# First-product weight operands: whole-unit loads into two rotating buffers, or piecewise loads into two fixed halves

## The chip, the cores and the metric

One Trainium2 chip, one of its cores. The metric is the device time of one launch in microseconds (us). TensorE is called PE here, VectorE DVE, ScalarE ACT, GpSimd POOL, and SyncE, which issues nearly all transfers of this kernel, SP.

## What is computed

Windowed attention over 4 x 8 heads of 576 x 64, whose output, as x of 2304 tokens x 512, goes through a mixture of 8 experts with Sinkhorn-normalised routing weights, and that through a feed-forward layer with the activation h cos(h). All in float32.

```python
attn = softmax(scale * q @ k.T + bias, causal window 128); x = attn @ v
P = exp(x @ w_gate - max)
for _ in range(8):
    P /= P.sum(1) + 1e-9
    P /= P.sum(0) + 1e-9
    P *= N / E
for e in range(8):
    out += P[:, e:e+1] * (relu(x @ w1[e]) @ w2[e])
h = out @ w_in
result = (h * cos(h)) @ w_out
```

## The kernel before, in words

The tokens are cut into three blocks of 768. After the attention the kernel runs 120 steps, one for each unit of 256 hidden columns in each block: 32 expert units for block 0, the same 32 for block 1 and for block 2 (kind "moe", b = 0, 1, 2), and 8 units of the feed-forward layer for each of the three blocks (kind "ffn").

Each unit has a first product (x by a slice of w1, or of w_in) and a second one (the hidden values by a slice of w2, or of w_out). The first product is a 2 x 2 block product in Strassen-Winograd form, with seven products numbered 1 to 7. `unit_mm` (L846) issues one of them: six matmuls of 128 x 384, since each operand is a pair of float32r numbers, high and low part, and three pairings are needed for each of two inner chunks. The left operands of the seven products, as high and low parts, are the tile `wa`: 14 KB in each partition, 1792 KB in all. The pool `wp` gives two buffers that rotate from unit to unit.

In block 0 the operands are made on the chip: `prep_s` (L126) forms four sums on POOL, `prep_a` (L136) copies the high parts on ACT, subtracts the low parts on DVE, and stores the whole tile into a DRAM scratch `wd1[u]` (L147). For the ffn units `prep_ffn` (L194) does the same in pieces during the later expert blocks and stores each piece into `wd1[u]` (L216). In blocks 1 and 2 and in all ffn steps, `wa` is loaded back from that scratch: `load_w(u, b, "a")` (L120), one transfer for a unit.

The order is written out by hand. The main loop (L1134) runs over the steps and within a step over the products in the order 5, 1, 4, 2, 3, 6, 7; at the place of product 4 the previous unit's product 4 is issued, which is its last. Right behind it `begin(n + 1)` (L1086) calls `load_w` for the next step, so that load waits until the previous unit's last product has read its buffer.

The second product of block 0 and of ffn is `g2` (L1064), 36 matmuls at the place marked 0 between products 6 and 7. For blocks 1 and 2 the second product is itself done in Strassen-Winograd form over pairs of units: `s_step` (L973) issues six matmuls behind each product (`couple`, L1026), and every second call issues on SP a load of 512 KB into one of the four parts of `wbX` (L1013), three products of that chain ahead. What it loads was made in block 0 by `prep_b` (L155) and `prep_sb` (L171), which forms the combinations of w2 on POOL (L181), splits them on ACT (L184) and DVE (L186) and stores them (L189). `prep_sb` is a generator: `slot()` (L1129, L1179, L1181) takes one piece of the first generator in the list `sbq`, which starts as `[prep_sb(0), prep_sb(1)]` (L1115); later units are appended by `begin_b` (L1098). A step of block 0 offers five slots, and five more in the batch of `g2` once there is one.

Behind the products, `product` (L862) drains the banks with ACT copies (`keep`, L881) and DVE additions (L884), and weighs the hidden values with the routing row by DVE (L899); that row is a broadcast load, one for four units (`load_p`, L797). The results of `s_step` are added up on DVE (L997) and its right operands split by ACT (L1009) and DVE (L1005). In blocks 1 and 2 the ffn weights are also converted in the background (`convert_f64`, L253, and `prep_ffn`), with loads and stores on SP.

SP issues its transfers in program order: one that waits for a semaphore holds those behind it.

## Time and profile before

| what | value |
|---|---|
| median of 3 runs | 2079.3 us (2074.7 to 2088.33) |
| the profiled execution's own time | 2079.26 us |
| its span | 2077.5 us |
| mean granted PE clock | 0.992 |
| PE busy | 2008.0 us |
| DVE, ACT, POOL busy | 1608.7, 869.5, 888.4 us |
| moved by transfers | 538.96 MB, mean 259 GB/s |

The span is what the profiler saw between first and last instruction. Busy time counts an engine as busy while an instruction of it is under way. [...] Block 0 lies between about 200 and 690 us of the span, block 1 from 700 to 1181, block 2 to 1670, the ffn stage behind.

### The profile page before, as it was taken

The page shows a single profiled execution, that of the slowest core. Times are in us where ns is not written, and L with a number is a line of the kernel's source. Part 1 is how long each engine was busy: PE and PEld are TensorE (multiplying, and loading weights), DVE is VectorE, ACT ScalarE, POOL GpSimd, SP SyncE. Part 2 cuts the span into 40 slices and gives each one's busy share as a digit, 9 for nine tenths or more (in the row PEclk, how much of TensorE's full clock was granted, in tenths as well). Part 3 has the DMA queues.
Part 4 walks back from the last instruction along what each step waited for, and adds up shares of the span by engine and source line. Part 5 has one row for each costly group of instructions (what it writes and reads, how often), then busy time and mean ns, then how long its engine had stood idle before and what let it go on. Part 6 is the DMA issues. An engine that isn't in the chain of part 4 may idle for free.

```text
span 2077.5 us, 30570 instructions
## 1 busy us (share of the span) xinstructions
PE 2008.0 (97%) x10960; PEld 1853.6 (89%) x10960; DVE 1608.7 (77%) x2714; ACT 869.5 (42%) x1639; POOL 888.4 (43%) x780
## 2 busy tenths in 40 slices
PE   8989899999999999999999999999999999999998
PEld 6656789989989899999999999999999998898897
DVE  6765787777777788878898878798887886857765
ACT  6776334444444343333333333233332345454443
POOL 5444356666657343343445332344352414223222
PEclk9999999999999999999999999999999999999999
DMA  6634578888888798878989678897888664455552
GB/s 162 189 69 120 209 274 297 306 314 296 308 309 304 254 336 314 316 281 322 327 312 338 261 270 291 301 336 282 333 319 279 240 244 184 170 218 198 203 188 107
DMA packets 236216, 538.96 MB, mean 259 GB/s; under 512 B 71872, under 2 KB 147744, under 8 KB 217632
## 3 DMA queue, kind: packets, MB, share of 16 engines
q1 hardware_dynamic: 236064, 537.00, 72.3%
q8 instruction: 87, 1.43, 0.3%
q14 instruction: 65, 0.53, 0.1%
HBM read 383.27 MB, written 153.67 MB: 258 GB/s over the span
## 4 chain that ended last, share of the span: by engine, by line
PE 81%; DVE 7%; DMA 7%; issue 2%; ACT 1%; POOL 1%; SPq 0%; POOLq 0%; ACTq 0%; DVEq 0%
PE gT L985 19%; PE y_moe L852 17%; PE z_moe L852 9%; PE gT L1073 6%; PE gT L1071 6%; PE gT L1072 6%; DMA wa<-wd 6%; PE y_ffn L852 4%; PE x_moe L852 4%; PE s L494 2%; PE z_ffn L852 2%; PE x L586 2%; PE x_ffn L852 1%; DVE hX L1005 1%; PE T L458 1%
## 5 line engine op out<-in xcount | busy, mean ns | idle before, releaser
L985 PE MATMUL gT<-hX,wbX 128*128 128x384 f32 x2688 | 543.0, 336 | 5.6 <-DVE acc_moe L997 3.1
L985 PEld LDWEIGHTS gT<-hX,wbX 128*128 128x128 f32 x2688 | 474.6, 189 | 10.8 <-DVE acc_moe L997 5.9
L852 PE MATMUL y_moe<-xtT_moe,wa 128*128 128x384 f32 x1728 | 347.0, 335 | 0.6 <-ACT s_moe L881 0.6
L852 PEld LDWEIGHTS y_moe<-xtT_moe,wa 128*128 128x128 f32 x1728 | 304.4, 188 | 3.3 <-ACT s_moe L881 0.9
L997 DVE TENSOR_TENSOR acc_moe<-gT,acc_moe 128x384 f32<-128x384 f32 x432 | 237.4, 550 | 88.7 <-PE gT L985 87.5
L1071 PE MATMUL gT<-wbX,hX 128*128 128x512 f32 x672 | 264.4, 393 | 8.2 <-ACT hX L802 4.3
L1073 PE MATMUL gT<-wbX,hX 128*128 128x512 f32 x672 | 264.4, 393 | 4.6 <-POOL hX L840 2.9
L1072 PE MATMUL gT<-wbX,hX 128*128 128x512 f32 x672 | 264.0, 393 | 0.0
L881 ACT ACTIVATE s_moe<-y_moe 128x384 f32<-128x384 f32 x192 | 93.5, 487 | 348.2 <-PE y_moe L852 348.2
L1018 POOL TENSOR_TENSOR cX<-cX 128x768 f32<-128x768 f32 x64 | 123.3, 1927 | 214.3 <-DVE hX L1005 125.6
L1018 POOL TENSOR_TENSOR hodd<-hodd 128x768 f32<-128x768 f32 x64 | 131.2, 2049 | 195.6 <-DVE hX L1005 109.7
L840 POOL TENSOR_TENSOR hX<-cX,hX 128x768 fp32r<-128x768 f32 x48 | 93.0, 1952 | 267.7 <-ACT hX L838 238.2
L133 POOL TENSOR_TENSOR s<-ra 128x256 f32<-128x256 f32 x80 | 61.5, 769 | 235.6 <-DVE wa L145 161.2
L1071 PEld LDWEIGHTS gT<-wbX,hX 128*128 128x128 f32 x672 | 127.2, 189 | 35.9 <-ACT hX L802 4.7
L1062 DVE SCALAR_TENSOR_TENSOR acc_moe<-gT,prob,acc_moe 128x512 f32<-128x512 f32 x174 | 129.9, 748 | 37.7 <-PE gT L1073 36.6
L1073 PEld LDWEIGHTS gT<-wbX,hX 128*128 128x128 f32 x672 | 127.0, 189 | 32.7 <-POOL hX L840 3.7
L1072 PEld LDWEIGHTS gT<-wbX,hX 128*128 128x128 f32 x672 | 127.2, 189 | 25.2
L1005 DVE TENSOR_TENSOR hX<-cX,hX 128x768 fp32r<-128x768 f32 x112 | 148.2, 1323 | 0.9 <-ACT hX L1009 0.9
L1005 DVE TENSOR_TENSOR hX<-hodd,hX 128x768 fp32r<-128x768 f32 x112 | 142.3, 1271 | 0.0
L852 PE MATMUL z_moe<-xtT_moe,wa 128*128 128x384 f32 x576 | 120.4, 343 | 21.8 <-DMA wa<-wd 16.5
L802 ACT ACTIVATE hX<-cX 128x768 fp32r<-128x768 f32 x64 | 44.0, 688 | 231.8 <-DVE cX L884 231.8
L852 PEld LDWEIGHTS z_moe<-xtT_moe,wa 128*128 128x128 f32 x576 | 102.7, 192 | 27.1 <-issue 7.3
(181 smaller groups left out, 3815.7 us busy)
## 6 DMA issues: line engine op xcount, KB each, us to landing
wa<-wd SPq DMA_DIRECT2D x88, 1792.0 KB, 7.4
wbX<-wdp SPq DMA_DIRECT2D x224, 512.0 KB, 8.0
wd<-wa SPq DMA_DIRECT2D x32, 1792.0 KB, 6.8
wdp<-sb SPq DMA_DIRECT2D x32, 1024.0 KB, 6.1
wdp<-wbX SPq DMA_DIRECT2D x96, 256.0 KB, 4.4
wbX<-wd SPq DMA_DIRECT2D x24, 1024.0 KB, 4.8
ra<-in_moe_w_dram SPq DMA_DIRECT2D x64, 256.0 KB, 7.4
rb<-in_moe_w_dram SPq DMA_DIRECT2D x64, 256.0 KB, 4.3
```

The lines of the kernel that those rows point to most:

```text
L133: nc.gpsimd.tensor_tensor(out=s4[:, o], in0=x, in1=y, op=op)
L840: nc.gpsimd.tensor_tensor(out=h[:, 1], in0=c, in1=h[:, 0].bitcast(F32), op=ALU.subtract)
L852: nc.tensor.matmul(ps[:, :HB], wa[:, wl, WI[m], kc, :], x[:, xl, kc, :], start=start and kc == 0 and n_ == 0, stop=stop and kc == 1 and n_ ...
L881: nc.scalar.activation(out=t["s", i], in_=ps[:, :HB], func=AF.Copy)
L985: nc.tensor.matmul(ps[:, :HB], w[:, u, wl, d * P:(d + 1) * P], x[:, xl, u, :], start=m in (1, 5, 2) and n_ == 0, stop=m in (4, 3, 2) and n ...
L997: nc.vector.tensor_tensor(out=a, in0=ps[:, :HB], in1=a, op=ALU.add)
L1005: nc.vector.tensor_tensor(out=x[:, 1], in0=H[:, q], in1=x[:, 0].bitcast(F32), op=ALU.subtract)
L1018: nc.gpsimd.tensor_tensor(out=H[:, t[0]], in0=H[:, t[1]], in1=H[:, t[2]], op=ALU.subtract)
L1062: nc.vector.scalar_tensor_tensor(out=a, in0=ps, scalar=pe, in1=a, op0=ALU.mult, op1=ALU.add)
L1071: nc.tensor.matmul(ps, hf[f][:, 0, ts], wb[:, f, 0, :], start=f == 0, stop=False)
L1072: nc.tensor.matmul(ps, hf[f][:, 0, ts], wb[:, f, 1, :], start=False, stop=False)
L1073: nc.tensor.matmul(ps, hf[f][:, 1, ts], wb[:, f, 0, :], start=False, stop=f == 1)
```

## The change

`wa` is no longer a rotating tile. One fixed tile `waX` holds two halves, for even and odd units, and each half holds the seven operands one after the other, with their high and low parts together (before: all high parts, then all low parts). The scratch in DRAM has the same order. A unit's operands are loaded in four transfers: those of products 5 and 1, of 2 and 3, of 6 and 7 (512 KB each) and of 4 (256 KB). When a product has been issued that frees the places of such a transfer, the transfer for the unit that uses this half next, two units on, is put down, and it is issued behind the product that follows. `begin` no longer loads. The operands of products 5 and 1 lie in places 3 and 0, of 2 and 3 in places 1 and 6, of 6 and 7 in 4 and 5, of product 4 in place 2. Besides, `prep_sb(1)` is not in the list from the start but appended at the beginning of the second step.

```diff
-    wp = ctx.enter_context(tc.tile_pool(name="wp", bufs=2))
+        waX = ring.tile([P, 2, 7 * 4 * P], F32R, name="waX")
-        def load_w(u, b, ab):
-            t = new_w(u, b, ab)
-            if ab == "a":
-                nc.sync.dma_start(out=flat_a(t), in_=wd1[u])
+        WI = {1: 0, 2: 1, 4: 2, 5: 3, 6: 4, 7: 5, 3: 6}
+        def wa_of(u):
+            return waX[:, u % 2].rearrange("p (o h k f) -> p o h k f", o=7, h=2, k=2)
+        def load_a(u, ms):
+            o = sorted(WI[m] for m in ms)
+            o = slice(o[0], o[-1] + 1, o[-1] - o[0] or 1)
+            out = waX[:, u % 2].bitcast(F32).rearrange("p (o w) -> p o w", o=7)
+            nc.sync.dma_start(out=out[:, o], in_=wd1[u].rearrange("p (o w) -> p o w", o=7)[:, o])
...
-            parts = [(wa[:, :, 0:2], both), (wa[:, :, 2], ra[:, 2:4, P:]), (wa[:, :, 3:7], s4)]
+            parts = [(wa[:, 0:2, 0], wa[:, 0:2, 1], both), (wa[:, 2, 0], wa[:, 2, 1], ra[:, 2:4, P:]),
+                     (wa[:, 3:7, 0], wa[:, 3:7, 1], s4)]
...
-            pieces = [(x, w1d[:, :, o], 2) for o, x in enumerate(ops)]
+            pieces = [(x, w1d[:, o], 2) for o, x in enumerate(ops)]
...
-                        ps[:, :HB], wa[:, wl, WI[m], kc, :], x[:, xl, kc, :],
+                        ps[:, :HB], wa[:, WI[m], wl, kc, :], x[:, xl, kc, :],
...
-                if b or kind == "ffn":
-                    load_w(u, b, "a")
-                elif u >= 2:
+                if kind == "moe" and not b and u >= 2:
                     pre.append(prep_a(u))
...
-        sbq += [prep_sb(0), prep_sb(1)]
+        sbq.append(prep_sb(0))
+        fetch = []
+        AHEAD = {1: (2, (5, 1)), 3: (2, (2, 3)), 7: (2, (6, 7)), 4: (1, (4,))}
...
+            if (kind, b, u) == ("moe", 0, 1):
+                sbq.append(prep_sb(1))
...
                     begin(n + 1)
                 else:
                     product(s, m)
+                while fetch:
+                    load_a(*fetch.pop(0))
+                if m in AHEAD:
+                    d, ms = AHEAD[m]
+                    if n + d < len(steps) and steps[n + d][:2] != ("moe", 0):
+                        fetch.append((steps[n + d][2], ms))
                 tick()
```

The loads of `wbX` for the ffn units move into a function `load_b` of their own, unchanged in place and size.

## Rows read from the trace of the kernel before

**Rows 1.** The page, busy time of PE: us, share of the span, instructions.

```profile
PE 2008.0 (97%) x10960; PEld 1853.6 (89%) x10960; DVE 1608.7 (77%) x2714; ACT 869.5 (42%) x1639; POOL 888.4 (43%) x780
```

**Rows 2.** Table: stretch, length, busy by engine, granted clock, DMA share, GB/s.

```profile
700.00:1181.00 481.00, 468.75 (x2638) 462.00 (x2637) 403.35 (x584) 164.13 (x291) 198.10 (x139) 0.98 0.84 311
...
286.00:680.00 394.00, 394.00 (x1985) 357.33 (x1984) 303.80 (x407) 174.46 (x284) 258.95 (x233) 1.00 0.86 306
1710.00:2050.00 340.00, 336.63 (x1685) 303.08 (x1684) 231.00 (x323) 166.52 (x251) 99.73 (x52) 1.00 0.52 188
```

**Rows 3.** Idle before wa's readers; PE's waits: us in total, times, longest.

```profile
  DMA wa<-wd: 17.0, 11
...
PE gT L985 <- DVE acc_moe L997: 3.1, 5, 1.0
...
PE gT L985 <- DMA wbX<-wdp: 0.5, 1, 0.5
```

**Rows 4.** Timelines of PE and SP, transfers of one window: two stalls, one load.

```profile
741.46 1.30 PE L852 MATMUL z_moe<-xtT_moe,wa 128*128 128x384 f32 x6 [0.89 <-DVE hodd L884]
...
1524.05 1.28 PE L852 MATMUL z_moe<-xtT_moe,wa 128*128 128x384 f32 x6 [0.93 <-DVE cX L899]
...
1513.79 0.32 SPq L120 DMA_DIRECT2D wa<-wd  x1
...
wa<-wd SPq DMA_DIRECT2D x1, 1792.0 KB, 10.1
```

**Rows 5.** SP's wait for wa; transfers: count, KB each, median us to landing.

```profile
SPq L120 <- PE y_moe L852: 314.7, 64, 11.3
...
wa<-wd SPq DMA_DIRECT2D x88, 1792.0 KB, 7.4
wbX<-wdp SPq DMA_DIRECT2D x224, 512.0 KB, 8.0
...
wd<-hla SPq DMA_DIRECT2D x48, 256.0 KB, 7.7
```

**Rows 6.** Timeline of PE around the longest stall: start, us, instructions, idle before.

```profile
843.65 1.34 PE L985 MATMUL gT<-hX,wbX 128*128 128x384 f32 x6 [0.97 <-DVE acc_moe L997]
844.83 1.20 PE L852 MATMUL y_moe<-xtT_moe,wa 128*128 128x384 f32 x6
845.87 1.20 PE L985 MATMUL gT<-hX,wbX 128*128 128x384 f32 x6
849.97 2.26 PE L852 MATMUL z_moe<-xtT_moe,wa 128*128 128x384 f32 x6 [2.90 <-DMA wa<-wd]
```

**Rows 7.** Table by stretch: the longest stall, first and last slow-clock stretches.

```profile
846.90:849.90 3.00, 0.17 (x1) 0.00 (x0) 3.00 (x4) 0.00 (x0) 1.80 (x1) 0.88 1.00 397
849.90:856.00 6.10, 6.03 (x19) 6.06 (x20) 1.61 (x3) 1.53 (x3) 0.73 (x1) 0.50 0.87 333
...
1401.00:1406.00 5.00, 5.00 (x20) 5.00 (x21) 1.79 (x4) 2.08 (x4) 0.00 (x0) 0.66 0.23 92
```

**Rows 8.** Timeline of SP: two ffn stores and a wa load.

```profile
831.19 0.54 SPq L216 DMA_DIRECT2D wd<-hlb  x1
...
834.19 0.53 SPq L216 DMA_DIRECT2D wd<-hla  x1
836.47 0.32 SPq L120 DMA_DIRECT2D wa<-wd  x1
```

**Rows 9.** Timeline of DVE: the same subtraction on runs of 256 and flat.

```profile
215.26 1.22 DVE L186 TENSOR_TENSOR sb<-sb 128x1024 fp32r<-128x1024 f32 x1 [0.25 <-ACT sb L184]
...
217.47 1.22 DVE L145 TENSOR_TENSOR wa<-s,wa 128x1024 fp32r<-128x1024 f32 x1
```

**Rows 10.** Timelines of SP, POOL and PE: the first units' combinations.

```profile
202.16 0.36 SPq L189 DMA_DIRECT2D wdp<-sb  x1
...
202.25 0.74 POOL L181 TENSOR_TENSOR sb<-rb 128x256 f32<-128x256 f32 x1 [10.55 <-DVE sb L186]
...
232.53 0.80 PE L1071 MATMUL gT<-wbX,hX 128*128 128x512 f32 x1 [4.30 <-ACT hX L802]
```

## The prediction

> **What bounds the kernel now.** I read the page's busy list first. TensorE (PE) is busy 2008.0 of a span of 2077.5 us [rows 1], so whatever the change does, it can only pay out of some 70 us of PE idle time and of stretches in which PE ran at less than its full clock. A table by stage then tells where these lie [rows 2]: the expert units of the first token block run without one idle microsecond (394.00 of 394.00), the cosine feed-forward stage nearly so (336.63 of 340.00), and the second block's experts lose 12.3 us in 481 (468.75). The third block loses as much again. So the two later expert blocks, about 970 us long, are where to look.

> The view of the tile wa names the cause there: the instructions that read it stood idle 17.0 us in 11 waits for the transfer into it [rows 3], ten of them at z_moe, the first product of an expert unit (product 5), one in the ffn stage. Three more stalls at the same instruction are put down to VectorE (0.89 us the first, 0.93 the last, 2.7 us the three together) [rows 4]. I do not believe that name: product 5 reads only wa and xt, and its bank had been free for longer. The wa load before the last of them was issued at 1513.79 and took 10.1 us to land, so 1523.9, and PE starts at 1524.05 [rows 4]; for the other two the same sum comes out. That makes 14 stalls, 19.7 us.

> Why is wa late only sometimes? Its load can be issued only when the last product of the previous unit has left the buffer: SyncE (SP) stands 314.7 us in 64 waits on that [rows 5]. In undisturbed stretches the groups of six matmuls start 1.04 us apart (844.83, 845.87) [rows 6], and from that point to the next unit's product 5 some ten groups run, 10.4 us. A wa load lands in 7.4 us in the median [rows 5], which fits; where the broadcast of the routing row and the conversions' transfers are in the queue as well it takes 10 or more, which does not.

> **What one stall costs.** Three terms. The idle time itself: 19.7 us. The end of the pipeline: the group before the stall ends at 845.87 + 1.20 = 847.07, while an undisturbed successor starts 1.04 after the start, so 0.16 us each [rows 6], 14 x 0.16 = 2.2 us. [...] A stretch of T us at a granted share g loses T x (1 - g): 6.1 x 0.50 = 3.05 for that one. There are four such stretches, all behind stalls of over 2 us; the last, 5.0 us at 0.66, loses 1.70 [rows 7], and the four together 9.0 us. All in all 19.7 + 2.2 + 9.0 = 30.9 us hang on late wa loads.

> **The loads, part by part.** Taken away: 88 loads of 1792 KB. Added: 4 for each of these 88 units, three of 512 KB (products 5 and 1, 2 and 3, 6 and 7) and one of 256 KB (product 4). Bytes are the same, issues rise by 264. Each is issued one product after the one that frees its place, for the unit two ahead. In groups of 1.04 us, 14 to a unit (a product and a step of the second product alternate): products 5 and 1 are loaded behind product 4, the third of its step, and needed at the first of the step two later, 28 - 4 = 24 groups, 25 us; the other three pieces have 24 to 27 us as well. The longest landing that the chain of PE's stalls met was under 14 us (836.47 issued, 849.97 started [rows 6, 8]). So all 14 stalls should go, even if the longest landing grew by two thirds. I take the 30.9 us as removed.

> What else is queued behind them. SP issues in program order, so each added load blocks SP until its product is done. The load of product pairs waits for a product two or three groups before the place where it is issued; the wbX load that follows it (second product, needed 12 groups on, 12.5 us) is free one group earlier. So a wbX load starts at most about 1 us later than without the piece, and lands in 8.0 us in the median [rows 5]: 12.5 - 8.0 - 1 leaves 3.5 us. Against this, today's single load holds SP for up to 11.3 us [rows 5] and lets wbX loads go in a burst; that wait goes. SP's issue time: 0.32 us for a wa load, 0.53 for a store with two pieces a row [rows 8], so 264 more issues are 84 to 140 us of SP, 1.0 to 1.6 us a unit of 15 us, on a queue that mostly stands in waits. Cost on PE: nothing; if the cover were gone (wbX late) each late load would cost what exceeds 3.5 us. The waits added ahead of products 4, 2 and 6 are met long before; the groups at 844.83 and 845.87, each behind met waits on a bank and an operand, are 1.04 apart all the same [rows 6], so they cost PE nothing.

> Smaller pieces a row: a load of 14 KB in one piece becomes rows of 2 KB twice, or 4 KB. The first-block stage moves pieces of 1 and 2 KB for the most part, the ffn stage rows of 14 and 8 KB; their rates for their share of the transfer engines are 306 / 0.86 = 356 and 188 / 0.52 = 362 GB/s [rows 2]. I take no cost; 2% of the 39% that wa has in the traffic (1.835 of 311 GB/s x 15.03 us = 4.67 MB) is below a hundredth.

> [...]

> **The new order in wa (product outermost)** changes three ScalarE copies and three VectorE subtractions of each first-block unit from flat to runs of 256 elements. The like operation on such runs (sb, 128x1024) and the flat one on wa take 1.22 us each [rows 9], so nothing; if it cost, the first block has VectorE busy 303.80 of 394 [rows 2] to hide it. Waits against single products in place of the whole buffer can only come earlier. 56 of the ffn preparation's stores get one run of 2 KB a row in place of two of 1 KB: under 0.2 us of SP each, hidden.

> **Second unit's combinations one unit later.** I expect no change at all. The first unit's generator gives way six times, the first step offers five slots, so the second already starts in the second step. The trace shows it: the first unit's store is issued at 202.16, and only then, at 202.25, GpSimd begins the next combinations [rows 10]. The changed code appends the generator to the same list before that slot is reached, so the order of instructions stays. The 4.30 us stall at 232.53 (ScalarE held behind it) stays too. If I miscounted, it is worth those 4.30 us either way.

> **What is late next.** With PE up to 2.9 us further on at each place, VectorE must follow. During the longest stall it had no pause (3.00 of 3.00) [rows 7], and 6 us earlier PE had waited 0.97 us for it [rows 6]. The bounds are nothing and such a wait at each place, 14 x (0.97 + 0.16) = 16 us. I charge it at three of the 14, 3.4 us, nearer to nothing because PE's waits on that line were 3.1 us in five over the whole 970 us [rows 3]. The sum: 30.9 - 3.4 = 27.5 us less. The profiled execution took 2079.26 us (span and 1.8 around it), the median of the runs is 2079.3, so both give 2051.8, said as **2052 us**, 1.3% less.

> **Rivals.**
> 1. VectorE takes the place of wa. For: busy 403 of 481 us [rows 2], full beside the longest stall. Against: the small sum of such waits [rows 3]. At its upper bound of 16 us, with a clock dip left at one or two places (3 us each), 31 - 16 - 3 = 12 us remain: 2067. It decides the sign only beyond its bound.
> 2. The wa loads stop binding but something of the same queue does, wbX or the routing row, in the same crowded moments. PE waited 0.5 us once on wbX in the whole run [rows 3], which speaks against. If half the stalls came back in that form: 2079 - 15 = 2064.
> 3. Slower: the transfer engines are taken by loads or pieces, not by bytes. Place: the two later blocks, at a share of 0.84 [rows 2], of which wa is 39%. If wa in pieces takes 1.5 times as long, the share is 0.84 x (1 + 0.39 x 0.5) = 1.00; from there it decides. At twice as long it is 1.17, units take 17% more over 970 us: 2079 + 165 = 2244. Against it stand the equal rates of the two stages.
> 4. The change doesn't do what it says: if places that lie apart (2 and 3 are slots 1 and 6) were tracked as one span, product 7 would wait for a load just issued, 7.4 - 1.0 = 6.4 us in each of 64 units, 2079 + 410 = 2490. Against: the ffn stores interleave in the same manner, land in 7.7 us, and are issued 3 us apart (831.19 and 834.19) [rows 8].

> **Chances.** Forecast 0.62 with its own range 2043 to 2060; rival 1 0.20, rival 2 0.09, rival 3 0.06, rival 4 0.03. The range 2042 to 2073 holds nearly the whole forecast and most of rivals 1 and 2, some 0.85. About 1% (21 us) is what a measurement of this kernel can tell from no change: the runs lie between 2074.7 and 2088.33. Under 2058.5 lie nine tenths of the forecast case and a sixth of rivals 1 and 2: 0.61. Slower by over 1%: rivals 3 and 4, 0.09. The rest, 0.30, lies within 1%.

> **What would show it.** Right: PE's waits on wa gone from the list; idle time in the stage 700 to 1181 down from 12 to about 4 us; no stretch at half clock there; wa loads landing with PE not near them; SP's long wait on y_moe split into short ones; the stall near 232 unchanged. Wrong: waits of L985 on wbX (rival 2), on acc_moe or hX from VectorE (rival 1), a DMA share near 1 at fewer GB/s (rival 3), y_moe waiting on wa in each unit (rival 4). A gain without the waits on wa gone would refute the account.

## The result, and the profile after

The changed kernel takes 2054.0 us in the median of six runs (2048.93 to 2055.85), the kernel before beside it 2080.98 (2074.7 to 2090.37): a ratio of 0.986, with a 95% interval of 0.9831 to 0.9888. The forecast was 2052 us. The profiled execution took 2048.93 us, 30.3 less than that of before (2079.26).

The page's busy line of the changed kernel, and its table by stage (the stretches of [rows 2]; the ffn stage begins some 30 us earlier, so its stretch is taken 30 us earlier). Columns as there: stretch, length, busy by engine, granted clock, DMA share, GB/s.

```profile
PE 1996.7 (98%) x10960; PEld 1845.7 (90%) x10960; DVE 1608.8 (79%) x2714; ACT 869.0 (42%) x1639; POOL 895.0 (44%) x780
```

```profile
286.00:680.00 394.00, 394.00 (x1984) 357.33 (x1983) 303.84 (x407) 174.37 (x283) 258.92 (x233) 1.00 0.85 303
...
700.00:1181.00 481.00, 477.00 (x2721) 471.00 (x2720) 420.11 (x605) 171.25 (x302) 206.66 (x141) 1.00 0.92 322
...
1680.00:2020.00 340.00, 336.63 (x1685) 303.06 (x1684) 231.02 (x323) 166.47 (x251) 99.78 (x52) 1.00 0.52 184
```

In the second block PE is idle 4.0 us where it was 12.3, at a granted clock of 1.00 (0.98 before; the share of its full clock that the profile lists as given to PE), and gets through 2721 matmuls in the same 481 us instead of 2638. The other two stages stand as they were. The transfer engines are busier for nearly the same bytes: 322 GB/s at a share of 0.92, against 311 at 0.84.

The whole difference lies in blocks 1 and 2 and the first steps of the ffn stage, as two stalls that both kernels have let one measure. First the kernel before, then the changed one (its lines are numbered one lower here), timelines of PE:

```profile
699.47 0.79 PE L1071 MATMUL gT<-wbX,hX 128*128 128x512 f32 x1 [2.49 <-DVE acc_moe L1062]
...
1717.08 0.50 PE L1073 MATMUL gT<-wbX,hX 128*128 128x512 f32 x1 [1.65 <-POOL hX L840]
```

```profile
699.38 0.79 PE L1070 MATMUL gT<-wbX,hX 128*128 128x512 f32 x1 [2.47 <-DVE acc_moe L1061]
...
1686.74 0.50 PE L1072 MATMUL gT<-wbX,hX 128*128 128x512 f32 x1 [1.65 <-POOL hX L840]
```

From the one stall to the other it is 1017.6 us before and 987.4 after, 30.3 less, which is all that the profiled execution gained. PE's idle time in between fell from 28.5 to 8.0 us, and what the lower clock cost, an estimate, from 11.5 to 1.3 us (the length of the stretch times what its mean granted clock, 0.989 and 0.999, lacks of 1).

PE's waits in the changed kernel (us in total, times, longest), SP's, and the transfers (count, KB each, median us to landing):

```profile
PE gT L1070 <- ACT hX L802: 4.2, 1, 4.2
PE gT L984 <- DVE acc_moe L996: 3.4, 5, 1.0
```

```profile
SPq L115 <- PE y_moe L851: 298.1, 155, 5.2
```

```profile
waX<-wd SPq DMA_DIRECT2D x264, 512.0 KB, 5.3
wbX<-wdp SPq DMA_DIRECT2D x224, 512.0 KB, 6.5
...
waX<-wd SPq DMA_DIRECT2D x88, 256.0 KB, 5.1
```

No wait of PE on the transfer into waX is left, where [rows 3] had 17.0 us. VectorE's place at the head of the list hardly grew (3.4 us in five waits; 3.1 in five before), and its and ScalarE's smaller places grew by 1.5 us together (hX at L1004 2.2 us for 1.3, s_moe at L880 1.2 for 0.6). SP's wait for the products came apart into short ones, 155 of them on y_moe, none over 5.2 us. Loads of wbX land 1.5 us sooner than in [rows 5].

At the place of the longest stall [rows 6] the changed kernel's timeline of PE reads:

```profile
841.85 1.32 PE L984 MATMUL gT<-hX,wbX 128*128 128x384 f32 x6 [0.96 <-DVE acc_moe L996]
843.61 1.32 PE L851 MATMUL y_moe<-xtT_moe,waX 128*128 128x384 f32 x6 [0.44 <-ACT s_moe L880]
844.77 1.21 PE L984 MATMUL gT<-hX,wbX 128*128 128x384 f32 x6
845.82 1.20 PE L851 MATMUL z_moe<-xtT_moe,waX 128*128 128x384 f32 x6
846.86 1.20 PE L984 MATMUL gT<-hX,wbX 128*128 128x384 f32 x6
```

The wait for VectorE ahead of it is still there (0.96 us, as 0.97 before), and then product 5 follows the step before it by 1.05 us, at a granted clock of 1.00 (mean of 841 to 850 us).

### The profile page after: what moved, and what is told of

The parts are those of the page before. It is cut to its first block, busy times and chain, and to the rows that moved or that the text cites. A ratio compares the mean times of both kernels' runs of the same rounds, so it can differ in the third digit from the quotient of the medians.

```text
span 2047.1 us, 31122 instructions
## 1 busy us (share of the span) xinstructions
PE 1996.7 (98%) x10960; PEld 1845.7 (90%) x10960; DVE 1608.8 (79%) x2714; ACT 869.0 (42%) x1639; POOL 895.0 (44%) x780
## 4 chain that ended last, share of the span: by engine, by line
PE 86%; DVE 8%; issue 2%; ACT 2%; DMA 2%; POOL 1%; SPq 0%; POOLq 0%; ACTq 0%; DVEq 0%
PE gT L984 21%; PE y_moe L851 18%; PE z_moe L851 9%; PE gT L1072 7%; PE gT L1070 6%; PE gT L1071 6%; PE x_moe L851 4%; PE y_ffn L851 4%; PE s L494 3%; PE z_ffn L851 2%; PE x L586 2%; PE x_ffn L851 1%; DVE hX L1004 1%; PE T L458 1%; PE pt L550 1%
## 5 line engine op out<-in xcount | busy, mean ns | idle before, releaser
L851 PE MATMUL y_moe<-xtT_moe,waX 128*128 128x384 f32 x1728 | 347.4, 335 | 1.2 <-ACT s_moe L880 1.2
L851 PEld LDWEIGHTS y_moe<-xtT_moe,waX 128*128 128x128 f32 x1728 | 304.2, 188 | 4.7 <-ACT s_moe L880 2.3
L880 ACT ACTIVATE s_moe<-y_moe 128x384 f32<-128x384 f32 x192 | 93.3, 486 | 336.0 <-PE y_moe L851 336.0
L1004 DVE TENSOR_TENSOR hX<-cX,hX 128x768 fp32r<-128x768 f32 x112 | 146.8, 1310 | 0.9 <-ACT hX L1008 0.9
L1004 DVE TENSOR_TENSOR hX<-hodd,hX 128x768 fp32r<-128x768 f32 x112 | 141.8, 1266 | 0.0
L851 PE MATMUL z_moe<-xtT_moe,waX 128*128 128x384 f32 x576 | 116.3, 335 | 2.4 <-DVE waX L145 2.3
L851 PE MATMUL z_moe<-xtB_moe,waX 128*128 128x384 f32 x576 | 115.9, 335 | 0.0
```

Of the source, the lines that this page charges most:

```text
L851: nc.tensor.matmul(ps[:, :HB], wa[:, WI[m], wl, kc, :], x[:, xl, kc, :], start=start and kc == 0 and n_ == 0, stop=stop and kc == 1 and n_ ...
L880: nc.scalar.activation(out=t["s", i], in_=ps[:, :HB], func=AF.Copy)
L1004: nc.vector.tensor_tensor(out=x[:, 1], in0=H[:, q], in1=x[:, 0].bitcast(F32), op=ALU.subtract)
```

## The experiments

All times are medians of runs made beside runs of the kernel before. The changed kernel, run again beside the second group, is the measure for the others:

> The changed kernel once more, as the measure for the kernels beside it on this chip: 2048 to 2056 us, 0.983 to 0.989 of the kernel before.

Measured: 2054.23 us (2050.39 to 2055.49), ratio 0.9878 (0.985 to 0.9906). Variants whose ratio lies near 0.986 are not told apart from the changed kernel here.

**In pieces, from the old place.** The change does two things at once: it splits the load, and it issues the parts for a unit further ahead. This puts the parts back to the place in the program where the one load stood.

```diff
                     begin(n + 1)
+                    if n + 1 < len(steps) and steps[n + 1][:2] != ("moe", 0):
+                        for ms in ((5, 1), (4,), (2, 3), (6, 7)):
+                            load_a(steps[n + 1][2], ms)
                 else:
                     product(s, m)
-                while fetch:
-                    load_a(*fetch.pop(0))
...
```

> The changed kernel, but all four loads of a unit are issued where the kernel before issued its one load: behind the last product of the unit before the running one, for the next unit. So the loads are in pieces, and not earlier. Theory A (a stall is lead against landing, piece by piece): product 5 now waits for the first 512 KB alone. Of the 10.1 to 13.4 us that the late whole loads took, the other 1280 KB are some 3.5 us at 370 GB/s, so the first piece lands in 6.6 to 9.9 us against a lead of 10.4: nearly all stalls go, PE's idle time on waX under 3 us, and the time is within 6 us of the changed kernel. Theory B (only the earlier issue pays): the stalls come back as before, 15 us and more on waX, and the time is within 8 us of the kernel before.

Measured: 2050.86 us (2048.94 to 2056.4), ratio 0.9866 (0.9848 to 0.9884). PE has no wait on waX. Table by stage and transfers:

```profile
700.00:1181.00 481.00, 476.76 (x2722) 470.83 (x2722) 423.28 (x605) 171.05 (x302) 203.84 (x141) 1.00 0.89 320
```

```profile
waX<-wd SPq DMA_DIRECT2D x264, 512.0 KB, 5.8
```

Theory A's forecast holds: the splitting gives all of it, and the issue two units ahead adds nothing that can be measured. But the place in the program does not fix the lead, and the theory's 10.4 us is not what the traces have. Leads are counted here to the place where PE would come to the product without a stall, from 0.32 us before the end of the issue, since SP can stand within an issue (0.32 us is the shortest issue of a load; the one at 832.22 below took 2.72). In the kernel before, the whole load has 9.2 us in the median of the 64 units of blocks 1 and 2. In this kernel the part of products 5 and 1 need not wait for product 4, as product 1 has freed its places, and SP issues it when its queue gets there: 13.9 us ahead in the median (8.7 to 19.3). It lands in 6.4 us in the median, the whole load in 7.5. So most first parts were smaller and earlier at once.

What the splitting does by itself is seen in five of the 16 units that follow a broadcast, where SP came to the first part only 8.7 to 9.9 us ahead. It landed in 7.8 to 8.4 us, and no stall followed; in the same five units of the kernel before the whole load took 10.1 to 13.4 us with leads of 9.1 to 10.6, and PE stood. One of the five is the place of the longest stall [rows 6, 8]; SP's issue and the start of product 5 in this kernel (the part landed at 842.4):

```profile
832.22 2.72 SPq L115 DMA_DIRECT2D waX<-wd  x1
```

```profile
844.56 1.20 PE L851 MATMUL z_moe<-xtT_moe,waX 128*128 128x384 f32 x6
```

In five others of the 16 the first part took 10.3 to 12.0 us, with leads of 13.6 to 13.9; whether these would have been in time with 9.2 us is not shown. The other half, whole loads issued earlier, would need a third buffer of 14 KB in each partition; it was not tried, so whether lead alone would do is open.

**How much lead the pieces need.**

```diff
-                while fetch:
-                    load_a(*fetch.pop(0))
+                for x in fetch:
+                    x[0] -= 1
+                while fetch and not fetch[0][0]:
+                    load_a(*fetch.pop(0)[1])
...
-                        fetch.append((steps[n + d][2], ms))
+                        fetch.append([10, (steps[n + d][2], ms)])
```

> The changed kernel with each load issued nine products later, so that its lead falls from 24 groups of 1.04 us to 6, 6.2 us. Theory A (lead against landing): 512 KB land in 5.3 us in the median, so a good part of the 64 units of blocks 1 and 2 waits at product 5, 2 or 6, by 1 to 4 us, with stretches of half clock behind: PE idle on waX 40 us or more, time 2085 to 2150. Theory B (it is the splitting and the shorter hold on SP that pay, the lead is of no matter): no waits on waX to speak of, time within 8 us of the changed kernel.

Measured: 2215.48 us (2210.42 to 2220.68), ratio 1.0654. PE's three longest waits on the transfer into waX:

```profile
PE x_moe L851 <- DMA waX<-wd: 52.5, 16, 7.0
PE x_ffn L851 <- DMA waX<-wd: 50.5, 21, 4.7
...
PE z_moe L851 <- DMA waX<-wd: 9.6, 7, 2.9
```

With two small ones PE's matmuls stood 115.4 us in 47 waits for waX. (The view of the tile gives 233.1 in 88, since it counts the weight loads that stood with the matmuls as well; in [rows 3] there were none of these.) PE idles 115.4 us more in the whole run than in the changed kernel, and the lower clock (a mean of 0.973 for 0.997) takes some 53 us more by the estimate above; together that is the 168 us between the two profiled executions.

Theory A in kind, but more than I had said. By the order of the program I counted a lead of six groups; it is five (two more products, and the steps of the second product between). The trace shows that SP's queue decides instead. In blocks 1 and 2 the part of products 5 and 1 has 9.6 us in the median but 3.9 at the least, that of products 2 and 3 (x_moe, which waited most) 9.7 and 4.4, as SP stands at loads of wbX before it comes to them (425.1 us in 168 waits for PE). In the ffn stage the four loads stand behind one of wbX that waits for the second product of an earlier unit, and the part of products 2 and 3 has 3.7 us in the median; 21 of 24 units wait there. So for products 5 and 1 the least lead is 20.5 us in the changed kernel, 8.7 with the pieces at the old place and 3.9 here; the first two give no stall on waX in blocks 1 and 2, and here there are 25. The limit lies where the landing times lie: 512 KB into waX land in 5.3, 5.8 and 6.6 us in the median of these three kernels.

**What made the whole load late: the broadcast.** The prediction put the stalls down to the routing row's broadcast and the conversions' transfers together. The broadcast is small, and lands later than a whole load of wa (7.4 us in the median [rows 5]); in the kernel before:

```profile
hX<-pT SPq DMA_DIRECT2D x16, 384.0 KB, 11.5
```

Two kernels made from the one before separate them. The first issues two broadcasts and no more:

```diff
             elif u % UPE == 0:
-                load_p((b - 1) * E + u // UPE + 1)
+                if (b, u) == (1, 0):
+                    load_p(1)
```

> The kernel before with only the first 2 of the 16 broadcasts of the routing row; the later units are weighed with an earlier expert's row. Theory: the broadcast is what makes the whole load of wa late every fourth unit; of the 14 stalls at product 5 at most 4 stay, idle time on wa under 6 us, time 2050 to 2060. Rival: the conversions' and the ffn preparation's transfers do it as well; two thirds or more of the stalls stay, time 2068 to 2080.

Measured: 2053.26 us (2051.31 to 2058.32), ratio 0.9884 (0.9849 to 0.992). PE's longest wait in blocks 1 and 2 and the second block's row:

```profile
PE gT L985 <- DVE acc_moe L997: 3.9, 6, 1.0
```

```profile
700.00:1181.00 481.00, 476.92 (x2724) 471.11 (x2724) 422.70 (x605) 171.14 (x302) 201.40 (x141) 1.00 0.85 313
```

With 14 of the 16 broadcasts gone, whole loads at their old place are in time, with the conversions and the ffn preparation running as before: 4.1 us idle in the second block, as in the changed kernel. One of the 14 stalls stays, the first of [rows 4], which has no broadcast near it and which the profile again puts down to VectorE:

```profile
740.14 1.28 PE L852 MATMUL z_moe<-xtT_moe,wa 128*128 128x384 f32 x6 [0.81 <-DVE hodd L884]
```

It is the meeting of broadcast and whole load that costs. The trace of the kernel before says the same, and more. Of its whole loads of blocks 1 and 2 issued between 700 and 1660 us, 49 had no broadcast beside them (in flight at the issue, or issued within the next 3 us); they landed in 6.8 to 9.3 us, the slowest three with three or four transfers of the conversions and the ffn preparation beside them. Of the 14 with a broadcast 13 landed in 9.3 to 13.4 us: 9.3 to 11.0 with none of those other transfers, 10.0 to 13.4 with some. So the broadcast is what it takes, and the conversions add to it. Why so small a transfer delays the load so much is not shown. The second kernel keeps all the broadcasts and moves each behind the next wa load:

```diff
                     begin(n + 1)
+                    if kind == "moe" and b and u % UPE == 1:
+                        load_p((b - 1) * E + u // UPE + 1)
...
-            elif u % UPE == 0:
-                load_p((b - 1) * E + u // UPE + 1)
```

> The kernel before, whole loads of 1792 KB at their old place, with one thing moved: the routing row's broadcast is issued behind the wa load of the next step instead of some two products ahead of it, at the end of the unit before. Theory (the stalls are this one meeting, the whole load queued behind the broadcast with 10.4 us to land): most of the 14 stalls go, idle before wa's readers under 6 us, time 2050 to 2062, as with the changed kernel. Rival (a broadcast anywhere near delays the load, since all share the transfer engines): half or more of the idle time stays or turns up as waits on wbX, time 2066 or more.

Measured: 2069.35 us (2065.1 to 2074.2), ratio 0.9945 (0.9924 to 0.9966). PE's longest wait, and the second block's row:

```profile
PE gT L985 <- DMA wbX<-wdp: 13.1, 12, 3.3
```

```profile
700.00:1181.00 481.00, 470.50 (x2671) 463.21 (x2670) 411.02 (x590) 167.17 (x296) 199.92 (x139) 0.99 0.85 315
```

The rival's forecast: product 5 no longer waits to speak of, as the theory said, but two thirds of the idle time turn up at the loads of wbX, which now come right behind both the whole load and the broadcast: 13.1 us in 12 waits. So a 1792 KB load and the broadcast next to each other make something late in either order of these two: 17.0 us of waits on wa [rows 3] in the one, 13.1 us on wbX in the other. That pieces help because loads of wbX can go between them is not shown: with the four pieces at the old place they stand together, and PE waited for wbX 1.5 us in three waits.

**How small the pieces may be.** 14 loads a unit, in rows of 1 KB:

```diff
-            nc.sync.dma_start(out=out[:, o], in_=wd1[u].rearrange("p (o w) -> p o w", o=7)[:, o])
+            src = wd1[u].rearrange("p (o w) -> p o w", o=7)
+            for m in ms:
+                for x in range(2):
+                    w = slice(x * 2 * P, (x + 1) * 2 * P)
+                    nc.sync.dma_start(out=out[:, WI[m], w], in_=src[:, WI[m], w])
```

> The changed kernel with 14 loads a unit of 128 KB in rows of 1 KB, at the same places, instead of 4. Theory A (lead against landing; small rows cost the transfer engines a little, which is hidden): no wait on waX, DMA share in block 1 up from 0.92 to 0.95 or so at about 320 GB/s, the time within 6 us of the changed kernel. Rival (the transfer engines are taken by loads or pieces, so that the share reaches 1): waits of PE on wbX or waX, GB/s in block 1 down, and a time of 2090 or more.

Measured: 2083.81 us (2077.1 to 2089.92), ratio 1.0021 (1.0007 to 1.0035): the whole gain is gone. PE's wait, the second block's row, and two of SP's waits:

```profile
PE gT L988 <- DMA wbX<-wdp: 20.4, 17, 4.7
```

```profile
700.00:1181.00 481.00, 462.69 (x2609) 453.64 (x2610) 397.20 (x580) 162.49 (x290) 195.64 (x137) 0.99 0.93 311
```

```profile
SPq L119 <- DMA wbX<-wdp: 75.3, 97, 1.8
SPq L119 <- DMA hX<-pT: 27.3, 12, 2.6
```

A miss for theory A, and not for the rival's reason either: the share is 0.93, hardly above the changed kernel's 0.92, and not 1. What has grown are SP's waits: at a load into waX it stands until a load into wbX or hX has landed with which it shares no data (in the changed kernel 3.1 us in five waits on wbX and 7.2 in four on hX), and the wbX loads behind it start late.

The trace tells which landing ends each of these waits: with SP's 2148 transfers counted in the order of their issue, that of the transfer eight issues before the load at hand. Here that is a broadcast, which landed at 1155.55; the load goes out at 1155.62, 0.07 us later:

```profile
1145.55 0.41 SPq L801 DMA_DIRECT2D hX<-pT  x1
...
1155.62 1.30 SPq L119 DMA_DIRECT2D waX<-wd  x3
```

Over all transfers of SP, waits that ended with the landing of the transfer eight issues before take 32.4 us in 49 in the kernel before, 56.0 in 91 in the changed one, and 224.3 in 313 here. Why it is the eighth is not shown.

Two kernels ask whether the number of loads or the short rows do that. One has seven loads of 256 KB in rows of 2 KB, the other the same seven from a scratch with high and low parts apart, in rows of 1 KB. The edits, the first against the changed kernel, the second against the first:

```diff
-            nc.sync.dma_start(out=out[:, o], in_=wd1[u].rearrange("p (o w) -> p o w", o=7)[:, o])
+            for m in ms:
+                nc.sync.dma_start(out=out[:, WI[m]], in_=wd1[u].rearrange("p (o w) -> p o w", o=7)[:, WI[m]])
```

```diff
-            out = waX[:, u % 2].bitcast(F32).rearrange("p (o w) -> p o w", o=7)
+            out = waX[:, u % 2].bitcast(F32).rearrange("p (o h w) -> p o h w", o=7, h=2)
+            src = wd1[u].rearrange("p (h o w) -> p o h w", o=7, h=2)
             for m in ms:
-                nc.sync.dma_start(out=out[:, WI[m]], in_=wd1[u].rearrange("p (o w) -> p o w", o=7)[:, WI[m]])
+                nc.sync.dma_start(out=out[:, WI[m]], in_=src[:, WI[m]])
...
-            w1d = wd1[u].rearrange("p (o h f) -> p o h f", h=2, o=7)
+            w1d = wd1[u].rearrange("p (h o f) -> p o h f", h=2, o=7)
```

> The changed kernel with one load of 256 KB for each of the seven products, rows of 2 KB, at the same places: 616 loads where the changed kernel has 352 and the 14-load kernel 1232. Count theory (SP is held at a load until an older one has landed, so what costs is the number of loads): SP begins to wait on landings of other loads, PE waits on wbX 1 to 6 us (20.4 with 14 loads), time 2052 to 2064. Row theory (what costs is the 1 KB row in the transfer engines): nothing changes, PE waits on wbX under 1 us, within 4 us of the changed kernel.

> As with seven loads, but the scratch in DRAM keeps high and low parts apart, so that each load moves rows of 1 KB, as the 14 loads did, at half their number. Count theory: the same time as with seven loads, within 4 us. Row theory: the same time as with 14 loads, 2076 to 2090, PE waiting on wbX 15 us or more.

Measured: 2049.55 us (2048.61 to 2050.51), ratio 0.9859 (0.9832 to 0.9885), and 2048.62 us (2047.6 to 2055.79), ratio 0.9862 (0.983 to 0.9893). The second block of the first and of the second, and SP's waits of the first:

```profile
700.00:1181.00 481.00, 477.85 (x2727) 472.41 (x2726) 424.48 (x607) 171.80 (x302) 205.23 (x141) 1.00 0.92 323
```

```profile
700.00:1181.00 481.00, 475.60 (x2712) 469.83 (x2712) 419.53 (x604) 170.88 (x301) 204.33 (x141) 1.00 0.94 322
```

```profile
SPq L114 <- DMA wbX<-wdp: 31.9, 37, 2.3
...
SPq L114 <- DMA hX<-pT: 15.8, 10, 2.8
```

(The second kernel also stores block 0's operands in two transfers a unit instead of one, which the edit above does not show.) The row theory falls: 1 KB rows raise the share to 0.94 and cost no time (2048.62 us against 2049.55). The count theory's cost for seven loads did not come either: PE has no wait on wbX, and the time is under its 2052 to 2064. What it said of SP did: the waits for the transfer eight issues before are 128.8 us in 260 with seven loads and 67.2 in 124 with their 1 KB rows. So with 352 and 616 loads into waX nothing is lost, and with 1232 PE pays; what is left as the cause is the number of loads (with it goes their size, 128 KB). How much of SP's loss then is its own issue time (0.38 us a load in the median) and how much the waiting was not separated. That seven loads came out 4.7 us under the changed kernel beside them is 0.2%; the next run shows how little that means.

**The second part alone.**

```diff
-        sbq += [prep_sb(0), prep_sb(1)]
+        sbq.append(prep_sb(0))
...
+            if (kind, b, u) == ("moe", 0, 1):
+                sbq.append(prep_sb(1))
```

> The kernel before with the second part of the change alone: the second unit's combinations appended at the second step. Theory: the instructions of every engine come in the same order as in the kernel before, so the time is the same within 0.3%, and the 4.3 us stall near 232 us stays. Rival (the edit is worth that stall): 4 us less and no stall there.

Measured: 2075.62 us (2072.16 to 2083.43), ratio 0.9978 (0.996 to 0.9995). The two programs have the same instructions in the same order on every engine, so this ratio is what the measurement gives for no change; its interval just misses 1, and differences of 0.2% should not be believed here. The stalls are there as before:

```profile
PE z_moe L852 <- DMA wa<-wd: 14.9, 8, 3.4
PE gT L1071 <- ACT hX L802: 4.5, 1, 4.5
```

**A try at the start.** The stall near 232 us, which the change leaves, comes from a ScalarE copy that waits for a store (7.64 us idle ahead of the copy at 230.93 in the changed kernel, ended by the store). Five empty turns put that copy behind the next unit's work:

```diff
             rb = raw_t[u, "b"]
+            for _ in range(5 if u == 2 else 0):
+                yield
```

> The changed kernel with five empty turns ahead of the third unit's combinations, so that the ScalarE copy that waits for the store of the second unit's combinations comes behind the next unit's hidden values. Theory: the stall near 232 us (4.2 us and about 3 us of half clock behind it) goes, the stretch 195 to 240 loses 5.8 us idle now and under 2.5 then; time 4 to 8 us under the changed kernel. Rival: the next waits of that start (VectorE's hidden values, the operands made by VectorE) take its place, gain under 2 us.

Measured: 2049.35 us (2047.72 to 2051.28), ratio 0.9856 (0.984 to 0.9873); its profiled span is 2046.9 us, the changed kernel's 2047.1. The table for 195 to 240 and 240 to 286, and the new wait:

```profile
195.00:240.00 45.00, 41.21 (x214) 36.88 (x214) 35.33 (x79) 19.51 (x33) 12.49 (x15) 1.00 0.41 144
240.00:286.00 46.00, 38.72 (x186) 33.35 (x185) 34.90 (x61) 16.45 (x28) 22.11 (x25) 0.96 0.78 273
```

```profile
PE gT L1072 <- DVE acc_moe L1053: 5.0, 3, 2.9
```

The rival wins: 195 to 240 does 28 matmuls more than the changed kernel's 186, and 240 to 286 does 16 fewer, held by VectorE. What is left is too small to measure: the ratio is 0.9856 where the changed kernel's is 0.986, each against the kernel before beside it. No version beat the changed kernel beyond the noise.

## Why the prediction was right

*What hangs on late wa loads, 30.9 us.* Right: 30.3 us went, all of it between the two stalls that enclose blocks 1 and 2, with the waits and the four stretches of lower clock gone (20.5 us of idle time and 10.2 us of clock, where the terms were 19.7 and 2.2, and 9.0). The clock's term, 3.05 us of it behind the longest stall, stands on the 6.10 us at a granted 0.50 of [rows 7]. The timeline of PE in the kernel before shows what that share does: the groups of six start 1.92 us apart there, and 1.04 apart before the stall [rows 6], so PE went at about half its pace:

```profile
852.03 2.12 PE L985 MATMUL gT<-hX,wbX 128*128 128x384 f32 x6
853.95 2.12 PE L852 MATMUL y_moe<-xtB_moe,wa 128*128 128x384 f32 x6
```

That the three stalls ascribed to VectorE were wa's too is borne out: they are gone while VectorE's work is the same.

*VectorE gives back 3.4 us.* Too much: on the line from which it was taken the waits grew by 0.3 us, VectorE's in all by 1.2 (and ScalarE's by 0.6). The place where it had no pause beside the longest stall was not a backlog that would last; this answers rival 1 too. Without this term the sum is 2048.4 and the profiled execution 2048.93. Between medians the gain is 27.0 us (2080.98 less 2054.0), so that the forecast of 27.5 hit the median so closely is in part luck.

*Lead of 24 groups and the longest landing under 14 us, so all stalls go.* The conclusion was right, and the lead as said (25.8 us in the median for products 5 and 1), but so long a lead was not needed. The pieces at the old place, with 13.9 us in the median and 8.7 at the least, do the same. The step compared the lead with the landing of the whole operand and did not ask what the first piece alone would need, although the 512 KB loads' row stood beside it.

*Why wa is late only sometimes.* Right in what it named, and not told apart: it takes the broadcast. The conversions and the ffn preparation add to it, and by themselves leave one stall of 0.81 us. The lead was mis-sized: 10.4 us count from the start of product 4, whose six matmuls have to end first (1.20 us [rows 6]), so it is 9.2.

*No cost of smaller rows.* Right for the time, wrong for the engines. 311 / 0.84 = 370 GB/s, an estimate for a full share, became 322 / 0.92 = 350 (357 in the second run of the changed kernel, 360 with the pieces at the old place), and 343 with seven loads of 1 KB rows. The comparison of two stages [rows 2] showed 356 and 362 and hid this, perhaps because they differ in more than rows. At shares of 0.92 and 0.94 it costs no time; no run shows it nearer to 1.

*Rival 3, priced by the share.* It did not come at four loads. At 14 loads the slowdown came by another way than the share: SP's queue. Loads of 512 and 256 KB cost this kernel no time (2054.0 us, and 2049.55 with seven loads of 256 KB); with loads of 128 KB (2083.81 us) it lost some 30 us against the larger pieces.

*Rivals 2 and 4.* Rival 4 is out, as no product waits for a load just issued. Rival 2 is not this kernel's case, but it is what happens when only the broadcast is moved (13.1 us of waits on wbX).

*Second part.* Right: no change, and the stall near 232 us stands:

```profile
232.41 0.79 PE L1070 MATMUL gT<-wbX,hX 128*128 128x512 f32 x1 [4.23 <-ACT hX L802]
```

## What to carry to other kernels

A load that is late only now and then is worth asking which other transfer it meets: leaving that one out for a run settled it here. Splitting a large load by the order of its use lets the first user wait for its own part, and lets that part set out when its own place is free; here that did what two units of lead also did. Measure a lead in the trace, from the issue to the user: what the issuing queue waits for before a load counts, not the load's place in the program (from the same place the whole load had 9.2 us here, the first part 13.9). And count the loads on that queue: in this kernel 1.75 times the changed kernel's number was free, and 3.5 times took the whole gain back.

## What the runs showed of the hardware that was not expected

A broadcast of 384 KB landed in 11.5 us in the median, and a load of 1792 KB beside it in 9.3 to 13.4 us (13 of 14), against 6.8 to 9.3 without it.

Rows of 2 and 4 KB in place of 14 KB raised the transfer engines' share in the second block from 0.84 to 0.92 (0.90 in the second run of that kernel, 0.89 with the pieces at the old place) with some 3% more moved in the same time, and rows of 1 KB to 0.94.

After the stall of 2.9 us PE ran at a granted clock of 0.50 for 6.1 us [rows 7] and got through 19 matmuls in them, which at the pace of [rows 6], six in 1.04 us, take 3.3 us; so that stall cost about twice its idle time, an estimate from these numbers. In the changed kernel the remaining waits of about 1 us in blocks 1 and 2 (0.96 us the one ahead of 841.85) were followed by no such stretch: the granted clock was 1.00 in both blocks.
